# Attention and the first expert layer in one written order, with rope tables built on the chip

## The chip, the cores and the metric

The kernel runs on one core of one Trainium2 chip. The metric is the device time of one execution in microseconds (us). Three runs of the kernel before gave 940.11, 942.00 and 943.37 us; their median is 942.0 us.

A core has five engines that work side by side, each on its own list of instructions in program order: PE multiplies matrices, DVE (VectorE) and ACT (ScalarE) do elementwise work, POOL (GpSimd) does elementwise work more slowly, and SP issues the transfers (DMAs). An instruction that has to wait holds up everything behind it on its engine, and nothing on the others. SBUF is the on-chip memory, PSUM the small memory that PE writes to.

## The reference

Three stages, cut to what is computed:

```
attention, 4 batches x 8 heads, 576 positions, head size 64:
    q, k = rope(q), rope(k)            # x*cos + swapped(x)*(-sin, sin), tables from the position
    attn = softmax(q k^T / 8);  a = attn v
first expert layer: x = a as [2304, 512]
    h = max(x w_in, 0);  x = (h*h) w_out        # w_in [512, 2048], w_out [2048, 512], float64
second expert layer, 8 experts of 512 x 1024 x 512:
    e = argmax(x w_gate + bias[modality]);  gate = its softmax weight
    out[t] = gate[t] * (max(x[t] w1[e], 0) w2[e])
```

## The kernel before, in words

Everything that PE multiplies is split into a high part and a low remainder, so that two or three passes give the precision of float32.

**Attention** (`attention`) works on 16 pairs of heads. For one pair p the steps have short names that the code looks up in the table `fs`:

- `ldq`, `ldk`, `ldv`: loads of q, k, v. q and k come with their halves swapped in a second plane. There is one buffer each for raw q and raw k, so the load of pair p+1 waits until pair p's raw data have been read for the last time.
- `aq`, `bq`, `cq` and `ak`, `bk`, `ck`: rope. Two multiplications with the tables `tab`, each 128x576, and an addition (function `rope`).
- `qh`, `ql`, `kh`, `kl0`, `kl1`: high parts (copies) and low remainders (subtractions). `qd0` to `qd2` and `kd0` to `kd2` move halves between the upper and lower 64 partitions, by a DMA or by a copy on an engine.
- `sc0` to `sc8`: nine tiles of scores on PE, in two PSUM slots. `mx0` to `mx8`: the row maximum of a tile on DVE. `ex0` to `ex8`: exp on ACT, which writes `e` and the row sums. So a score tile waits until the exp of two tiles earlier has left its slot.
- `tr..` and `ev..`: 128x128 transposes of `e` on PE, and the copies that take them out of PSUM. `trrr`, one transpose of the reciprocal row sums, is the only instruction of line 303 and occurs once in a pair. `sa` and `srec` make those reciprocals.
- `pv0`, `pv1`, `u0`, `u1`: attention times v on PE, 20 matmuls each, and the copies of its result; `sev`, `rst`, `rld`, `xn`, `xh`, `xl`, `xr`, `xst` divide by the row sums and store x in DRAM.

**The first expert layer** (`experts`) runs 5 blocks of up to 512 tokens by 16 chunks of 128 hidden columns: `m1` (12 matmuls, `mm1`), `re`, `sq`, `gg`, `gl` (relu, square and remainder on ACT and DVE) and `m2` (12 matmuls, `mm2`). The weights are float64 in DRAM. Each of 32 half chunks i is loaded (`wd`) and turned into two float32 parts by `wx` (ACT, two instructions), `wy` (DVE, two), `wz` (POOL), `wb` (DVE), `wh` (ACT) and `wl` (DVE or POOL). There are four raw buffers and four buffers for the intermediate.

**The order.** Within a pair, tables of due times (`FIRST`, `SECOND`, `THIRD`, `PLAN`, one for pair 0, 1, 2 and 3, and 4 to 15) give each step a time and an engine; a pair's times are shifted by 18 for each pair, and all steps are sorted by time. `TAIL` adds most weight steps of half chunks 0 to 11 and the `m1` of chunks 1, 0 and 2 and the `m2` of chunk 0. From there a loop over units takes over: it emits the `m1` of two chunks ahead, the weight steps of a fixed number per unit (`Weights.slot`) and then the `m2` of its chunk.

At the start the program issues rawk, tabk, rawq and tabq in two halves each, sets whole buffers to zero on POOL (lines 399 to 402), and begins pair 0.

Of the kernel before, what the change touches and what calls it, by code (L numbers as in the profile page):

```python
# [1241 lines left out]
```

## Time and profile before

| | |
|---|---|
| median of three runs | 942.0 us (940.11 to 943.37) |
| the profiled execution's own time | 943.84 us |
| its span, first to last instruction | 942.0 us |
| mean granted TensorE clock | 0.991 of full speed |
| PE busy | 889.0 us, 94% of the span |
| DVE busy | 629.7 us, 67% |
| ACT busy | 471.8 us, 50% |
| POOL busy | 321.3 us, 34% |
| moved by DMA | 122.44 MB |

The busy shares are means over stages with different limits. PE's idle time is 53 us, and the rows below show in which stretches it lies. A profile's times count from the first instruction; what the execution takes beyond its span is 1.84 us.

### The profile page before, as it was taken

The page shows a single profiled execution, that of the slowest core. Times are in us where ns is not written, and L with a number is a line of the kernel's source. Part 1 is how long each engine was busy: PE and PEld are TensorE (multiplying, and loading weights), DVE is VectorE, ACT ScalarE, POOL GpSimd, SP SyncE. Part 2 cuts the span into 40 slices and gives each one's busy share as a digit, 9 for nine tenths or more (in the row PEclk, how much of TensorE's full clock was granted, in tenths as well). Part 3 has the DMA queues.
Part 4 walks back from the last instruction along what each step waited for, and adds up shares of the span by engine and source line. Part 5 has one row for each costly group of instructions (what it writes and reads, how often), then busy time and mean ns, then how long its engine had stood idle before and what let it go on. Part 6 is the DMA issues. An engine that isn't in the chain of part 4 may idle for free. (4 is left out here: it accounts for less than half of the span.)

```text
span 942.0 us, 14580 instructions
## 1 busy us (share of the span) xinstructions
PE 889.0 (94%) x5210; PEld 746.4 (79%) x5210; DVE 629.7 (67%) x1151; ACT 471.8 (50%) x929; POOL 321.3 (34%) x251
## 2 busy tenths in 40 slices
PE   1799999999999999999999999999999999999995
...
GB/s 242 130 158 168 213 176 199 184 201 169 173 104 230 89 183 177 144 102 9 1 79 56 1 1 85 6 1 20 26 202 45 118 230 260 228 224 238 203 92 35
DMA packets 50672, 122.44 MB, mean 130 GB/s; under 512 B 10960, under 2 KB 15072, under 8 KB 50592
## 3 DMA queue, kind: packets, MB, share of 16 engines
...
q8 instruction: 43, 0.70, 0.3%
...
HBM read 93.45 MB, written 15.54 MB: 116 GB/s over the span
## 5 line engine op out<-in xcount | busy, mean ns | idle before, releaser
L665 ACT ACTIVATE r<-h 128x512 f32<-128x512 f32 (+1 forms) x80 | 44.3, 553 | 224.7 <-PE h L659 212.1
L659 PE MATMUL h<-xs,w 128*128 128x512 f32 (+1 forms) x660 | 144.8, 368 | 2.2 <-DVE w L516 2.0
L673 DVE SCALAR_TENSOR_TENSOR h<-h,r 128x512 f32<-128x512 f32 (+1 forms) x80 | 51.6, 644 | 133.3 <-ACT r L665 133.3
L659 PEld LDWEIGHTS h<-xs,w 128*128 128x128 f32 x660 | 115.5, 188 | 25.4 <-DVE w L516 3.7
L270 ACT ACTIVATE e<-sc,nmx 128x576 f32<-128x576 f32 x144 | 106.2, 739 | 54.6 <-DVE nmx L259 53.5
L259 DVE TENSOR_REDUCE nmx<-sc 128x1 f32<-128x576 f32 x144 | 106.7, 753 | 35.6 <-PE sc L254 31.6
L254 PE MATMUL sc<-kh,q 128*128 128x288 f32 (+1 forms) x336 | 98.7, 330 | 33.7 <-ACT q L185 19.2
L693 PE MATMUL y<-w,gh 128*128 128x512 f32 x396 | 122.6, 391 | 0.0
L254 PEld LDWEIGHTS sc<-kh,q 128*128 128x128 f32 x336 | 62.8, 195 | 50.8 <-ACT e L270 24.6
L931 DVE TENSOR_TENSOR w<-eraw,w 128x1024 fp32r<-128x1024 f32 x64 | 78.4, 1225 | 33.8 <-ACT w L930 33.8
L254 PE MATMUL sc<-kl,q 128*128 128x288 f32 (+1 forms) x336 | 90.3, 304 | 0.0
L312 PE MATMUL b<-ident,e 128*128 128x128 f32 x640 | 84.4, 279 | 3.9 <-ACT e L270 3.3
L693 PEld LDWEIGHTS y<-w,gh 128*128 128x128 f32 x396 | 73.3, 188 | 14.4
L580 POOL TENSOR_TENSOR xraw<-xraw,rbs 128x512 f32<-128x512 f32 (+1 forms) x14 | 16.6, 1185 | 196.8 <-DMA rbs<-rD 190.7
L312 PEld LDWEIGHTS b<-ident,e 128*128 128x128 f32 x640 | 75.6, 144 | 4.9 <-ACT e L270 3.7
L693 PE MATMUL y<-w,gl 128*128 128x512 f32 x198 | 77.1, 389 | 0.0
L977 PEld LDWEIGHTS h<-ye,w 128*128 128x128 f32 x576 | 74.0, 189 | 3.7
L977 PE MATMUL h<-ye,w 128*128 128x256 f32 x576 | 74.8, 280 | 0.0
L1000 PE MATMUL y<-w,ge 128*128 128x512 f32 x288 | 74.6, 394 | 0.0
L341 PE MATMUL b<-et,v 128*64 128x288 f32 x512 | 70.0, 412 | 1.0 <-DVE et L187 0.8
...
L930 ACT ACTIVATE w<-eraw 128x1024 fp32r<-128x1024 f32 x64 | 67.3, 1052 | 4.2 <-DMA eraw<-wexp 4.2
(219 smaller groups left out, 1714.4 us busy)
## 6 DMA issues: line engine op xcount, KB each, us to landing
...
```

The lines of the kernel that those rows point to most:

```text
L254: nc.tensor.matmul(out=o[:, x:x + w], lhsT=q[:, hd, q0:q0 + 128], rhs=k[:, hd, y:y + w], start=(n == 0), stop=(n == len(ops) - 1))
L259: nc.vector.tensor_reduce(out=m, in_=sc(p, j)[:, :, 0:HS], axis=AX.XY, op=ALU.max, negate=True)
L270: nc.scalar.activation(out=e(p)[:, o:o + S].rearrange("p (a b) -> p a b", a=2), in_=sc(p, j)[:, :, 0:HS], func=ACTF.Exp, bias=live[p, f"nm ...
L312: nc.tensor.transpose(t[:, i * 128:(i + 1) * 128], x[:, o:o + 128], ident)
L341: nc.tensor.matmul(out=o[64 * hd:64 * hd + 64], lhsT=lhsT, rhs=rhs, start=(c == 0), stop=(c == 4))
L659: nc.tensor.matmul(out=h, lhsT=w[:, a, k * 128:(k + 1) * 128], rhs=xs[b, k][:, c], start=(k == 0 and i == 0), stop=(k == 3 and i == 2))
L673: nc.vector.scalar_tensor_tensor(out=h, in0=h, scalar=W_SC, in1=rs[n], op0=ALU.mult, op1=ALU.mult)
L693: nc.tensor.matmul(out=yp[t], lhsT=g[a][:, t * 128:(t + 1) * 128], rhs=w[:, c, 512:1024], start=(f == 0 and i == 0), stop=(f == NFC - 1 an ...
L930: nc.scalar.activation(out=w[:, 0], in_=r, func=ACTF.Copy)
L931: nc.vector.tensor_tensor(out=w[:, 1], in0=r, in1=f32(w[:, 0]), op=ALU.subtract)
L977: nc.tensor.matmul(out=h, lhsT=w[:, a, k * 128:(k + 1) * 128], rhs=x[:, c], start=(k == 0 and i == 0), stop=(k == 3 and i == 2))
L1000: nc.tensor.matmul(out=yp[s, t], lhsT=g[a][:, t * 128:(t + 1) * 128], rhs=w[:, c, 512:1024], start=(f == 0 and i == 0), stop=(f == EFC - 1 ...
```

## The change

The due-time tables are gone. In their place stands one list, `ORDER`, of 1590 words such as `5.kl0.V`: pair, step and engine, in the order in which they are emitted. Pair 16 stands for the expert layer. The list goes on past attention through all 32 weight half chunks, the `m1` of chunks 0 to 13 and the `m2` of chunks 0 to 11, and the loop over units starts at unit 12 (`HQ`). In the list the `m1` are in the order 4, 1, 0, 2, 3, 5, 7 ahead of the first `m2`, where before three `m1` stood ahead of it.

The rope tables come as one quarter, `tabs`, 64 partitions by 2x576 (288 KB where four transfers of 288 KB were), and the other three quarters are made by four instructions `tab0` to `tab3`, two on DVE and two on ACT. At the start only those parts of the buffers are set to zero that nothing else writes.

The head of the list, and what reads it:

```diff
-        plan = [(t + p * PERIOD, p, name, eng) for p in range(NP)
-                for name, (t, eng) in (FIRST, SECOND, THIRD, THIRD, PLAN)[min(p, 4)].items()
-                if (p or name not in ("ldk", "ldq")) and (p < 4 or name not in BLOCK0)]
-        for t, p, name, eng in sorted(plan, key=lambda z: z[0]):
+ORDER = """
+0.tab2.A 0.tab3.A 0.tab1.V 0.tab0.V 0.ak.V 0.bk.V 0.ck.V 0.aq.V 0.bq.V 0.cq.V 0.kh.A 0.qh.V 0.kd1.A 0.kd0.A 0.ql.V
...
+        for word in ORDER.split():
+            p, name, eng = word.split(".")
+            if int(p) < NP:
+                fs[name](int(p), eng)
+                continue
+            if name in ("open", "bank", "ring"):
+                {"open": early, "bank": banks, "ring": ctx}[name].close()
+            tail(name, eng)
```

```diff
+        def tables(p, eng, n):
+            t = tab["k"][LO]
+            o, i = ((tab["k"][UP, :, 64:S], t[:, :, 0:512]), (tab["k"][UP, :, 0:64], t[:, :, 512:S]),
+                    (tab["q"][LO], t), (tab["q"][UP], t))[n]
...
+        nc.sync.dma_start(out=tab["k"][LO], in_=tabs)
         for x in "kq":
             for c in range(2):
                 nc.sync.dma_start(out=raw(0, x)[:, c], in_=src[x][0, :, c])
-                nc.sync.dma_start(out=tab[x][:, c], in_=table[x][:, c])
-            nc.gpsimd.memset(f32(kl_buf[i]), 0.0)
-            nc.gpsimd.memset(f32(q_buf[i]), 0.0)
+            nc.gpsimd.memset(f32(kl_buf[i][UP, 0]), 0.0)
+            nc.gpsimd.memset(f32(kl_buf[i][LO, 1]), 0.0)
```

Of the buffers, the second `e` moves out of the pool that is closed early, the PSUM of the score tiles is given up at the word `bank`, after the last exp, and the `wb` of odd half chunks writes to SBUF where before, in the loop, it wrote to a PSUM bank.

Three places show what moves. The first is ACT at the start of the program; `tabq<-tabk` builds a table, `wmag<-wraw` and `wraw<-wraw` are weight steps (`wx`), the rest is pair 0. Before:

```order
L483 ACT_TABLE_LOAD
L483 ACTIVATE wmag<-wraw 128x512
L484 ACTIVATE wraw<-wraw 128x512
L185 ACTIVATE kh_85<-rawk 128x576
L185 ACTIVATE kh_85<-kh_85 64x576 x2
L185 ACTIVATE q_83<-rawq 128x576
L185 ACTIVATE q_83<-q_83 64x576
L483 ACTIVATE wmag<-wraw 128x512
L484 ACTIVATE wraw<-wraw 128x512
L185 ACTIVATE kh_85<-kh_85 64x576
L185 ACTIVATE q_83<-ql 64x576
```

Now:

```order
L219 ACT_TABLE_LOAD
L219 ACTIVATE tabq<-tabk 64x1152 x2
L190 ACTIVATE kh_85<-rawk 128x576
L190 ACTIVATE kh_85<-kh_85 64x576 x3
L190 ACTIVATE q_83<-q_83 64x576
L190 ACTIVATE q_83<-ql 64x576
```

No weight step stands ahead of pair 0 any more; two table instructions do.

The second place is POOL in one pair in the middle of attention (`rawq`, `rawk`: rope; `ql`, `kl`: remainders; `e`: `sa`; `wf`: a weight step). Before, one pair takes nine rows:

```order
L201 TENSOR_TENSOR rawq<-rawq,tabq 128x576 x2
L203 TENSOR_TENSOR rawq<-rawq 128x576
L516 TENSOR_TENSOR wf<-wmag,wf 128x512
L190 TENSOR_TENSOR ql<-rawq,q_84 128x576
L201 TENSOR_TENSOR rawk<-rawk,tabk 128x576
L278 TENSOR_SCALAR e_90<-e_90 128x9
L201 TENSOR_TENSOR rawk<-rawk,tabk 128x576
L203 TENSOR_TENSOR rawk<-rawk 128x576
L190 TENSOR_TENSOR kl_88<-rawk,kh_86 64x576
```

Now:

```order
L206 TENSOR_TENSOR rawq<-rawq,tabq 128x576
L206 TENSOR_TENSOR rawq<-rawq 128x576
L486 TENSOR_TENSOR wmag<-wmag,wraw 128x512
L195 TENSOR_TENSOR ql<-rawq,q_84 128x576
L206 TENSOR_TENSOR rawk<-rawk,tabk 128x576 x2
L206 TENSOR_TENSOR rawk<-rawk 128x576
L507 TENSOR_TENSOR wf<-wmag,wf 128x512
```

One rope multiplication of q, the remainder `kl` and `sa` have left POOL.

The third place is DVE at the same point of a pair, between two row maxima (`nmx`) of its scores. Before:

```order
L259 TENSOR_REDUCE nmx<-sc 128x1 x4
L190 TENSOR_TENSOR kl_88<-rawk,kh_86 64x576
L259 TENSOR_REDUCE nmx<-sc 128x1
L187 COPY xo<-b 128x288
L259 TENSOR_REDUCE nmx<-sc 128x1
```

Now:

```order
L271 TENSOR_REDUCE nmx<-sc 128x1 x2
L192 CAST kh_85<-rawk 128x576
L192 COPY rs<-b 9x128
L195 TENSOR_TENSOR kl_87<-rawk,kh_85 64x576
L271 TENSOR_REDUCE nmx<-sc 128x1 x2
L206 TENSOR_TENSOR rawq<-rawq,tabq 128x576
L490 SCALAR_TENSOR_TENSOR wmag<-wraw,wmag 128x512
L195 TENSOR_TENSOR kl_87<-rawk,kh_85 64x576
L490 SCALAR_TENSOR_TENSOR wmag<-wraw,wmag 128x512
L271 TENSOR_REDUCE nmx<-sc 128x1 x2
L192 CAST q_84<-rawq 128x576
```

What left POOL has come to DVE, with the copies `kh` and `qh` from ACT; from DVE to ACT went one copy of 128x288 and some of the transposes' copies.

## Rows read from the trace of the kernel before

**Rows 1.** The page: busy times, and the 40 slices of PE
```profile
PE 889.0 (94%) x5210; PEld 746.4 (79%) x5210; DVE 629.7 (67%) x1151; ACT 471.8 (50%) x929; POOL 321.3 (34%) x251
...
PE   1799999999999999999999999999999999999995
```
**Rows 2.** Busy time by stage: stretch, length, each engine's us and instructions, clock, DMA
```profile
0.00:19.20 19.20, 0.00 (x0) 0.03 (x1) 5.82 (x9) 8.37 (x13) 10.04 (x13) 1.00 0.68 229
19.20:128.30 109.10, 98.18 (x713) 81.13 (x714) 92.61 (x132) 79.77 (x189) 83.44 (x62) 0.97 0.60 173
128.30:293.10 164.80, 157.20 (x1216) 126.80 (x1215) 139.97 (x215) 120.66 (x281) 113.09 (x87) 0.99 0.59 171
293.10:300.10 7.00, 6.01 (x43) 3.04 (x41) 5.50 (x10) 2.29 (x5) 4.14 (x3) 1.00 0.73 226
300.10:420.00 119.90, 115.67 (x501) 93.22 (x501) 91.29 (x154) 67.18 (x117) 52.45 (x37) 1.00 0.48 154
420.00:900.00 480.00, 479.62 (x2585) 413.45 (x2584) 284.61 (x623) 182.91 (x310) 52.30 (x46) 1.00 0.32 101
```
**Rows 3.** Timeline of the start: begin, length, engine, line, idle time before it
```profile
6.21 1.39 POOL L201 TENSOR_TENSOR rawk<-rawk,tabk 128x576 f32<-128x576 f32 x1
6.75 1.47 DVE L201 TENSOR_TENSOR rawk<-rawk,tabk 128x576 f32<-128x576 f32 x1 [5.73 <-DMA tabk<-tabk]
8.32 0.76 DVE L203 TENSOR_TENSOR rawk<-rawk 128x576 f32<-128x576 f32 x1
...
10.16 0.78 DVE L201 TENSOR_TENSOR rawq<-rawq,tabq 128x576 f32<-128x576 f32 x1 [1.09 <-DMA tabq<-tabq]
...
11.94 0.66 ACT L483 ACTIVATE wmag<-wraw 128x512 f32<-128x512 f32 x1 [9.91 <-DMA wraw<-wio]
...
13.05 0.67 ACT L185 ACTIVATE kh<-rawk 128x576 fp32r<-128x576 f32 x1
13.75 1.39 ACT L185 ACTIVATE kh<-kh 64x576 fp32r<-64x576 f32 x2
14.56 1.40 POOL L190 TENSOR_TENSOR kl<-rawk,kh 64x576 fp32r<-64x576 f32 x1 [4.23 <-ACT kh L185]
...
16.55 0.74 DVE L190 TENSOR_TENSOR kl<-rawk,kh 64x576 fp32r<-64x576 f32 x1
...
17.32 0.46 DVE L187 CAST q<-ql 64x576 fp32r<-64x576 f32 x1
...
19.20 0.58 PE L254 MATMUL sc<-kh,q 128*128 128x288 f32 x1 [19.20 <-ACT q L185]
```
**Rows 4.** Timeline of PE: four of the 16 instructions of line 303
```profile
128.33 0.27 PE L303 MATMUL b<-ident,e 128*128 128x128 f32 x1
...
196.65 0.27 PE L303 MATMUL b<-ident,e 128*128 128x128 f32 x1
...
212.19 0.27 PE L303 MATMUL b<-ident,e 128*128 128x128 f32 x1
...
293.14 0.27 PE L303 MATMUL b<-ident,e 128*128 128x128 f32 x1
```
**Rows 5.** Groups of DVE by shape, 100 to 250 us: count, busy us, mean ns, idle before
```profile
L259 DVE TENSOR_REDUCE nmx<-sc 128x1 f32<-128x576 f32 x81 | 60.0, 755 | 13.2 <-PE sc L254 9.8 <-ACT rs L185 1.4
L187 DVE COPY et<-b 128x512 f32<-128x512 f32 x36 | 24.6, 684 | 0.6 <-PE b L312 0.2
L190 DVE TENSOR_TENSOR kl<-rawk,kh 64x576 fp32r<-64x576 f32 x9 | 13.7, 1522 | 0.3
L187 DVE COPY et<-b 128x256 f32<-128x256 f32 x18 | 6.3, 390 | 0.0
L187 DVE COPY xo<-b 128x288 f32<-128x288 f32 x10 | 4.5, 450 | 0.9 <-PE b L341 0.8
```
**Rows 6.** Groups of POOL by shape, 100 to 250 us
```profile
L201 POOL TENSOR_TENSOR rawq<-rawq,tabq 128x576 f32<-128x576 f32 x17 | 24.2, 1443 | 0.0
```
**Rows 7.** Timeline of DVE near the end of attention: one weight step's first instruction
```profile
294.57 0.73 DVE L488 TENSOR_SCALAR wmag<-wmag 128x512 f32<-128x512 f32 x1
```
**Rows 8.** Who waited for whom on PE, 20 to 420 us: total, times, longest
```profile
PE sc L254 <- ACT e L270: 14.2, 14, 2.2
...
PE h L659 <- DVE w L516: 2.0, 4, 0.6
```

More of the change, by code (lines that the diff above doesn't have):

```diff
@@ L36, in f32 @@
     return ap.bitcast(F32)
-PERIOD = 18
-PLAN = {
[20 rows of a table removed]
-}
-FIRST = {
[20 rows of a table removed]
-}
-SECOND = {
[21 rows of a table removed]
-}
-THIRD = {
[21 rows of a table removed]
-}
-TAIL = {
[26 rows of a table removed]
-}
-def attention(tc, qx, kx, v, tabq, tabk, ident, eye, xT, rD, ps, tail=None):
+ORDER = """
+0.tab2.A 0.tab3.A 0.tab1.V 0.tab0.V 0.ak.V 0.bk.V 0.ck.V 0.aq.V 0.bq.V 0.cq.V 0.kh.A 0.qh.V 0.kd1.A 0.kd0.A 0.ql.V
+0.kd2.A 0.qd0.A 0.kl0.V 0.qd1.A 0.sc3.T 0.mx3.V 0.kl1.P 0.sc0.T 0.mx0.V 16.wd0.D 0.ex3.A 1.ldq.D 1.ldk.D 0.ex0.A
+16.wd6.D 16.wd4.D 0.ldv.D 1.ldv.D 16.wd1.D 0.sc2.T 1.bq.P 0.qd2.V 0.sc7.T 0.mx2.V 0.mx7.V 1.aq.V 0.ex2.A 0.ex7.A
@@ new lines @@
+0.sc4.T 1.cq.P 0.sc1.T 0.mx4.V 0.ex4.A 0.mx1.V 0.sc6.T 0.ex1.A 1.qh.A 1.ak.V 1.bk.V 0.mx6.V 1.qd0.A 1.ck.P 0.ex6.A
+0.sc5.T 0.mx5.V 1.ql.V 1.qd1.V 1.kh.A 0.ex5.A 1.kd1.A 0.trm02.T 1.kd0.V 0.trm03.T 0.trm00.T 1.kd2.A 0.sc8.T 0.mx8.V
+1.kl0.P 0.trrk.T 0.ex8.A 0.evrk.V 0.evm02.V 1.kl1.P 1.sc1.T 1.sc3.T 0.evm00.A 0.evm03.A 1.mx1.V 1.ex1.A 1.mx3.V
+0.trm13.T 1.ex3.A 0.sa.P 0.trm12.T 16.wx0.A 1.sc2.T 0.srec.V 0.evm13.V 0.evm12.V 0.trrr.T 0.trm11.T 1.mx2.V 2.ldq.D
+1.ex2.A 1.sc0.T 1.qd2.D 0.trm10.T 1.sc6.T 0.evrr.A 1.mx0.V 2.ldk.D 1.ex0.A 0.evm11.A 1.sc5.T 2.aq.P 2.bq.P 0.trm01.T
@@ new lines @@
+1.trm02.T 2.cq.V 2.ak.V 2.bk.P 1.mx6.V 1.mx5.V 2.qh.A 0.sev.A 2.ck.V 2.ql.V 1.ex6.A 2.qd0.D 3.ldq.D 1.evm02.A
+0.evm01.V 2.kh.A 1.ex5.A 2.kd1.A 1.trm03.T 1.sc8.T 2.kl0.P 1.mx8.V 2.kd0.V 1.ex8.A 2.qd1.D 0.trrq.T 0.evm10.V 0.evrq.A
+2.kl1.P 1.trm00.T 1.sc4.T 1.sc7.T 1.mx7.V 2.kd2.D 0.rst.D 16.wy0.V 3.ldk.D 2.qd2.D 1.ex7.A 0.pv0.T 1.mx4.V 1.ex4.A
+1.evm03.V 2.sc2.T 1.sa.V 2.mx2.V 3.aq.P 3.bq.P 1.srec.V 1.evm00.A 0.u0.A 2.ex2.A 1.trrq.T 2.sc1.T 3.cq.V 3.ak.V 3.bk.P
+1.trm01.T 1.trm12.T 2.sc3.T 0.pv1.T 3.qh.A 1.evm01.A 2.mx1.V 2.mx3.V 3.ck.V 2.ex1.A 3.ql.V 2.ex3.A 0.rld.D 3.qd0.D
@@ new lines @@
+2.sc7.T 1.evrq.V 4.ldq.D 16.wz0.P 2.sc6.T 1.trm10.T 1.evm12.A 3.kh.A 1.trm11.T 3.kd1.A 2.mx7.V 2.mx6.V 3.kl0.P 2.ex7.A
+2.sc4.T 1.trrr.T 2.ex6.A 3.kd0.V 2.sc0.T 3.qd1.D 1.evm11.A 0.u1.A 2.mx4.V 2.ex4.A 1.trm13.T 2.mx0.V 2.ex0.A 1.trrk.T
+3.kl1.P 3.kd2.D 2.sc5.T 4.aq.V 1.evm10.A 2.sc8.T 1.evrr.A 2.mx5.V 0.xr.D 2.trm01.T 1.evm13.V 4.bq.P 2.mx8.V 3.qd2.D
+1.sev.V 4.ldk.D 2.ex5.A 4.cq.P 2.evm01.A 2.ex8.A 3.sc2.T 2.trm13.T 3.mx2.V 4.qh.V 2.trm12.T 2.evm13.V 2.trm02.T
+3.ex2.A 3.sc1.T 1.evrk.A 2.sa.P 2.evm02.A 3.sc3.T 3.mx1.V 4.qd0.D 2.trrq.T 2.trm11.T 3.mx3.V 2.trm00.T 3.ex1.A
@@ new lines @@
+2.evm12.V 2.evm11.V 4.ql.P 2.srec.V 2.ldv.D 4.bk.P 3.ex3.A 3.sc7.T 5.ldq.D 4.ak.P 2.trrk.T 3.sc6.T 2.evrq.A 2.trrr.T
+3.mx7.V 16.wb0.V 4.ck.P 3.mx6.V 2.evrk.A 1.pv1.T 3.ex7.A 16.wx1.A 4.kh.V 2.evrr.V 3.sc4.T 3.ex6.A 1.u1.A 3.sc0.T
+1.pv0.T 4.kd1.D 3.mx4.V 16.wx4.A 4.qd2.D 3.ex4.A 4.kd0.A 3.mx0.V 3.ex0.A 0.xn.P 4.kl0.V 3.sc5.T 5.aq.V 3.sc8.T 0.xh.A
+4.kl1.V 3.mx5.V 1.u0.V 4.kd2.D 3.trm01.T 4.qd1.A 5.bq.P 3.mx8.V 2.trm10.T 5.ldk.D 3.ex5.A 2.sev.A 5.cq.P 2.evm00.V
+3.evm01.A 3.ex8.A 2.evm10.A 4.sc3.T 2.trm03.T 3.trm13.T 5.qh.V 4.mx3.V 4.sc2.T 3.trm12.T 4.ex3.A 3.evm13.V 3.trm02.T
@@ new lines @@
+2.evm03.A 4.sc1.T 3.sa.P 3.evm02.A 1.rst.D 5.qd0.D 3.trrq.T 3.trm11.T 4.mx2.V 3.trm00.T 3.evm12.V 4.mx1.V 3.evm11.V
+5.ql.P 3.srec.V 3.ldv.D 1.rld.D 5.bk.P 4.ex2.A 2.rst.D 6.ldq.D 5.ak.P 4.ex1.A 3.trrk.T 4.sc0.T 3.evrq.A 3.trrr.T
+16.wy4.V 4.sc4.T 2.pv1.T 5.ck.P 4.mx0.V 4.mx4.V 4.ex0.A 3.evrk.A 4.ex4.A 5.kh.V 3.evrr.V 0.xl.V 5.kd1.D 0.xst.D
+5.qd2.D 5.kd0.A 16.wh0.A 4.sc5.T 5.kl0.V 4.sc6.T 4.mx5.V 4.mx6.V 2.pv0.T 4.ex5.A 6.aq.V 5.kl1.V 4.ex6.A 5.kd2.D 2.u0.A
+5.qd1.A 4.sc7.T 6.bq.P 4.ldv.D 3.trm10.T 6.ldk.D 1.xn.V 3.sev.A 6.cq.P 2.rld.D 4.sc8.T 3.evm00.V 4.mx7.V 2.u1.V
@@ new lines @@
+2.xh.A 6.kd1.D 6.qd2.D 2.xl.V 6.kd0.A 5.sc5.T 6.kl0.V 5.sc6.T 5.mx5.V 5.mx6.V 2.xst.D 3.pv0.T 1.xr.D 5.ex5.A 4.pv0.T
+7.aq.V 16.wy2.V 6.kl1.V 5.ex6.A 6.kd2.D 4.u1.A 3.u0.A 6.qd1.A 5.sc7.T 7.bq.P 5.ldv.D 4.rst.D 4.u0.A 7.ldk.D 7.cq.P
+3.rld.D 5.sc8.T 5.mx7.V 3.u1.V 5.trm00.T 4.xr.D 5.trm01.T 5.ex7.A 5.evm00.A 6.sc3.T 5.mx8.V 5.trm13.T 5.trm10.T 7.qh.V
+5.evm01.A 5.trrk.T 6.mx3.V 5.ex8.A 6.sc2.T 5.evm13.V 6.ex3.A 5.trm12.T 5.evrk.A 6.sc1.T 5.trrq.T 5.trm11.T 7.qd0.D
+5.evm10.V 6.mx2.V 5.sa.V 6.mx1.V 5.srec.V 5.trm03.T 7.ql.P 5.evm12.A 7.bk.P 5.trm02.T 6.ex2.A 5.evrq.A 8.ldq.D 7.ak.P
@@ new lines @@
+6.trrq.T 6.trm11.T 8.qd0.D 6.evm10.V 7.mx2.V 6.sa.V 7.mx1.V 6.srec.V 6.trm03.T 8.ql.P 6.evm12.A 8.bk.P 6.trm02.T
+7.ex2.A 6.evrq.A 9.ldq.D 8.ak.P 7.ex1.A 6.evm02.A 6.evm11.V 6.trrr.T 7.sc0.T 6.evm03.V 7.sc4.T 6.evrr.V 8.ck.P 7.mx0.V
+7.mx4.V 7.ex0.A 7.ex4.A 16.wz2.P 8.kh.V 6.sev.V 6.pv1.T 8.kd1.D 16.wb2.V 8.qd2.D 8.kd0.A 7.sc5.T 8.kl0.V 7.sc6.T
+7.mx5.V 7.mx6.V 16.wd5.D 7.ex5.A 6.pv0.T 9.aq.V 16.wx6.A 8.kl1.V 7.ex6.A 8.kd2.D 6.u1.A 8.qd1.A 7.sc7.T 9.bq.P
+16.wy6.V 7.ldv.D 6.rst.D 6.u0.A 9.ldk.D 9.cq.P 7.sc8.T 7.mx7.V 7.trm00.T 6.xr.D 7.trm01.T 7.ex7.A 7.evm00.A 8.sc3.T
@@ new lines @@
+7.mx8.V 7.trm13.T 7.trm10.T 9.qh.V 7.evm01.A 7.trrk.T 8.mx3.V 7.ex8.A 8.sc2.T 7.evm13.V 8.ex3.A 7.trm12.T 7.evrk.A
+8.sc1.T 7.trrq.T 7.trm11.T 9.qd0.D 7.evm10.V 8.mx2.V 7.sa.V 8.mx1.V 7.srec.V 7.trm03.T 9.ql.P 7.evm12.A 9.bk.P
+7.trm02.T 16.wl4.P 8.ex2.A 7.evrq.A 10.ldq.D 9.ak.P 8.ex1.A 7.evm02.A 7.evm11.V 7.trrr.T 8.sc0.T 7.evm03.V 8.sc4.T
+7.evrr.V 9.ck.P 8.mx0.V 8.mx4.V 8.ex0.A 8.ex4.A 9.kh.V 7.sev.V 7.pv1.T 16.wx5.A 9.kd1.D 9.qd2.D 9.kd0.A 16.wh2.A
+8.sc5.T 9.kl0.V 8.sc6.T 8.mx5.V 8.mx6.V 8.ex5.A 7.pv0.T 10.aq.V 9.kl1.V 8.ex6.A 9.kd2.D 16.wy5.V 7.u1.A 9.qd1.A
```

191 lines of the change are left out of this document (123 added, 68 removed), and 108 rows, old and new, of tables (FIRST, PLAN, SECOND, TAIL).

## The prediction

> **What bounds the kernel now.** I read the page first. PE is busy for 889.0 of 942.0 us, and its slices show where it is not: hardly in the first of 40, half in the last, full in between [rows 1]. The last lies behind everything that the change touches. So the change can win only where PE idles ahead of it, and it can lose wherever another engine becomes slower than PE.
>
> Next I cut the span into stages [rows 2]. PE starts at 19.20. From there to the row-sum transpose of the sixth pair (128.33) it idles 109.1 - 98.2 = 10.9 us, over the next ten pairs 164.8 - 157.2 = 7.6 us, and from 300.1 to 420 another 4.2 us. From 420 to 900 it idles 0.4 us of 480, and that stretch keeps its code.
>
> A busy PE can still be slow, so I looked at one instruction that comes once in a pair [rows 4]. From 196.65 to 212.19 a pair took 15.54 us; I use this as PE's floor. The ten pairs up to 293.14 took 164.81 / 10 = 16.48 us each, so 0.94 us of a pair can be won by order. Ten pairs held 1216 matmuls [rows 2], 121.6 each, which makes 15.54 / 121.6 = 0.128 us a matmul. The 713 matmuls of the stretch before would then need 91 us, and took 109.
>
> Who holds PE up is the softmax chain: score tiles waited 14.2 us for the exp that frees their slot, 14 times, up to 2.2 us; exp in turn follows the row maximum on DVE [rows 8, 5]. DVE is busy for 92.6 of 109.1 us and 140.0 of 164.8 us, 85% of both stretches [rows 2]. It is the next bound behind PE, and the question for the new order.
>
> **The start.** Before, three things lie in front of the first score [rows 3]. The rope multiplications wait for the fourth transfer (6.75) and the eighth (10.16). ACT sits idle for 9.91 us in front of a weight step whose data come at 11.94; two such instructions run, and `kh`, whose data were done at 8.32 + 0.76 = 9.1, begins at 13.05. Then high parts, remainders and moves follow each other until 19.20.
>
> Now the loads are five halves of the old size. Four transfers took 10.16 - 6.75 = 3.41 us, 0.85 each, which puts the table at 6.75 - 3 x 0.85 = 4.2 and the last half of q at 7.6. Then on DVE: `tab1` and `tab0`, which no row shows. A one-input instruction over 512 elements took 0.73 [rows 7], and `tab0` has 1024: between 0.73 and 1.46, I take 1.0, and 0.25 for the small `tab1`, so 5.45. Six rope instructions at 0.76 give 10.0, `qh` 0.46 (as the cast of 576 elements at 17.32), `ql` and `kl0` 0.74 each [rows 3]: 11.95. ACT has the two q tables done at 4.2 + 2 x 1.4 = 7.0 (twice the 0.70 of half the 1.39 row), before `aq` needs them at 7.7; then `kh`, three moves, `qd0` and, behind `ql`, `qd1` end at 11.9. On POOL `kl1` runs 1.40 beside the rope work, and a DVE multiplication beside POOL took 1.47 where others took 0.78 [rows 3]: 0.7 more. First score at 12.7, bounds 11.95 and, with all six rope instructions at 1.47, about 17. That is 6.5 us gained; the weight steps that leave come back later on ACT, which is 73% busy there [rows 2]. The smaller zeroing takes POOL off this path altogether. Since `1.ldq` waits for `ql` of pair 0, pair 1 moves forward with it.
>
> **First score to the sixth pair's row-sum transpose.** PE's work ahead of this point is the same but for 4 matmuls. On DVE I counted the words: 27 two-input instructions on SBUF where 14 were, 12 more casts, 5 copies of transposes and one result copy fewer. That is 13 x 0.75 + 12 x 0.46 - 5 x 0.684 - 0.45 = +11.4 us [rows 3, 5], so 104 us of work where 92.6 us were; POOL loses 10 x 1.443 = 14 us [rows 6]. An engine that idled 16.5 us would idle 5. The order can fill PE's holes only as far as DVE lets it; I leave this stretch at 109.1 us, with 97 (PE's 91 and 6 for the first pair, whose tiles can only go at the pace of the exps) and 118 as ends.
>
> **The next ten pairs.** DVE's work is 140.0 / 10 = 14.0 us a pair. It gains `kl0` and `aq` (0.75 each) and `qh` and `kh` (0.46 each), and loses two copies of 0.390 and one of 0.450: +1.2, so 15.2 us, below PE's 15.54. But in this stage `kl1` took 1.522 us [rows 5] and not 0.74. With `kl0` and `aq` at that price it is 16.7 us. POOL, which gives up three of its instructions in a pair, will be in the way less often, so I take the middle, 16.0, and with little idle time left a period of 16.2 us: 10 x (16.48 - 16.2) = 2.8 us gained. Ends: 15.54 and 17.9 (below). ACT rises from 120.7 / 10 = 12.1 us by less than 1.5 and stays hidden.
>
> The row for `kl1` is also where the Trainium skill bears on the case. Its page "SBUF — State Buffer", section "Who interferes with whom", says that a VectorE instruction with two SBUF inputs and a GpSimd instruction that reads SBUF exclude each other: the one that comes second waits for the whole of the first. By that rule `kl0` and `aq` could each wait for a full POOL instruction of 1.443 us, and a pair would come to 15.2 + 2 x 1.44 = 18.1 us, slower than now; at half such a wait it is 16.6. The trace agrees that the two collide (1.522 against 0.74), and its mean extra of 0.78 is near the half.
>
> **The end of attention and the first layer.** I keep the 7.0 us from the last row-sum transpose to the first `m1` [rows 2]. Of the 4.2 us idle up to 420, 2.0 are four waits for weights behind DVE [rows 8]; seven `m1` ahead of the first `m2` give the weight steps some 20 us of cover, so I take 2.0 us off. If DVE had no room here, these waits would come back, 0.6 us each. The remaining weight steps are the same in number.
>
> **Sum.** 12.7 + 109.1 + 162 + 7.0 = 290.8 where 300.1 stood: -9.3, and -2.0 in the first layer: -11.3. The profiled span of 942.0 becomes 930.7; with the 1.84 us outside the span the profiled execution would go from 943.84 to 932.5. The median of the runs equals the span's figure, so I predict 931 us.
>
> **Rivals.**
>
> 1. *PE becomes the only bound.* DVE's collisions go with POOL's load, and the row maxima come when wanted. Then 12.7 + 97 + 155.4 + 7.0 = 272.1, 28 less, and 3 less in the first layer: 911 us. For it: PE did hold 15.54 for single pairs. Against it: DVE would then have to be busy for over 97% of each pair.
>
> 2. *The early start is eaten.* The first pairs are set by DVE, ACT and the arrival of pair 1's data; the new rope work on DVE takes what the start gave, and the stretch grows by the same 6.5 us. Only 2.8 + 2.0 remain: 937 us. For it: the 11.4 us more on DVE just there. Against it: 16.5 us of idle time to put them in.
>
> 3. *DVE becomes the bound (slower).* The place is the middle of attention, behind `kh`, where POOL begins the next pair's rope work while DVE does `kl0`, `aq` and `kl1`. With `kl0` and `aq` at 1.522 and the two casts at twice 0.46 a pair needs 14.0 + 1.2 + 1.54 + 0.92 = 17.7 us, 17.9 with a little idle time; the 13 new instructions of the first stretch at that price make 114 us of work, 118 with idle time. 12.7 + 118 + 179 + 7.0 = 316.7: 16.6 more, 958 us. It decides from a period of 16.48 + 8.5 / 10 = 17.3 us, where start and first layer are paid back. For it: `kl1` in that stage. Against it: POOL has less to do, and its next additions wait for DVE's own results.
>
> **How the numbers follow.** A measurement of this kernel can tell about 0.3% (2.8 us) from no change. My forecast gets 0.40, with a range of its own of 922 to 939; rival 1 gets 0.18, rival 2 0.20, rival 3 0.22. Faster than 939.2: all of rival 1, nearly all of the forecast and two thirds of rival 2, 0.70. Within 0.3%: 0.10. Slower: nearly all of rival 3, 0.20. The range runs from 913 to 950: it leaves out the better half of rival 1 and the worse half of rival 3.
>
> **What would show it.** The first score near 12.7, with no idle time of ACT in front of `kh` but for DVE's rope work. Row-sum transposes 16.2 us apart after the sixth pair; 15.6 would speak for rival 1, over 17.3 for rival 3. DVE's `kl` and `rawq` groups near 1.1 us; at 1.5 rival 3 has its price. DVE busy for over 95% of 109 us in the first stretch. No wait of PE for `w` behind DVE in the first layer. I am wrong altogether if the first score comes after 17, or if another wait (a load held up in SP's queue, a PSUM bank not yet copied out) takes the place of the one on exp; the trace would then show PE idle with that releaser.

## The result: slower, and where

The changed kernel takes 952.54 us (median of 4 runs, 952.28 to 955.74), where the kernel before took 942.68 beside it: ratio 1.011, interval 1.007 to 1.015. I had predicted 931. The profiled span is 950.5 us, 8.5 more than before.

The page of the changed kernel, first the busy times, then PE's 40 slices and its granted clock (to be read beside [rows 1]):

```profile
PE 894.2 (94%) x5210; PEld 749.3 (79%) x5210; DVE 649.4 (68%) x1213; ACT 483.9 (51%) x956; POOL 263.1 (28%) x201
...
PE   3899989898999997799999999999999999999995
...
PEclk9999999999999999799999999999999999999998
```

The first slice is fuller than before, as forecast. But slices 16 and 17 show 7 where [rows 1] have 9, and in the second of them the clock falls to 0.7. Cut into stages (the columns of [rows 2], the first four stages and then the first expert layer in three parts):

```profile
0.00:13.10 13.10, 0.00 (x0) 0.00 (x0) 9.00 (x21) 7.70 (x9) 4.15 (x9) 1.00 0.48 158
13.10:123.60 110.50, 100.72 (x709) 81.42 (x710) 97.80 (x151) 84.04 (x195) 61.93 (x44) 1.00 0.58 173
123.60:293.70 170.10, 159.29 (x1220) 127.75 (x1219) 156.13 (x252) 132.73 (x310) 96.20 (x67) 0.99 0.55 161
293.70:298.90 5.20, 5.20 (x43) 2.83 (x41) 3.47 (x10) 3.19 (x6) 1.05 (x1) 1.00 0.63 233
298.90:374.00 75.10, 74.04 (x326) 60.67 (x324) 53.58 (x83) 45.96 (x82) 30.14 (x23) 1.00 0.40 130
374.00:386.00 12.00, 0.97 (x2) 0.54 (x2) 9.37 (x14) 3.27 (x6) 5.50 (x4) 0.61 0.24 71
386.00:430.00 44.00, 43.37 (x181) 34.83 (x182) 27.92 (x57) 13.38 (x23) 7.02 (x5) 0.95 0.44 136
```

Against [rows 2]: the start is 6.1 us shorter (13.1 for 19.2), the stretch to the sixth pair 1.4 longer (110.5 for 109.1), the next ten pairs 5.3 longer (170.1 for 164.8), the end of attention 1.8 shorter (5.2 for 7.0). So the first `m1` comes only 1.2 us earlier than before, and everything behind it takes 950.5 - 298.9 = 651.6 where it took 942.0 - 300.1 = 641.9: 9.7 us lost, more than the whole difference. In this trace most of it lies in one place: from 374 to 386 PE does 0.97 us of work in 12.

The waits of PE, 10 to 430 us (total, times, longest; [rows 8] before), name it:

```profile
PE sc L266 <- ACT e L282: 18.7, 24, 2.4
...
PE y L685 <- ACT w L504: 11.1, 1, 11.1
PE h L649 <- DVE gl L667: 1.2, 2, 1.0
```

The timeline of the changed kernel around that wait, with rows of ACT, DVE, POOL and PE (begin, length, what ended the idle time before):

```profile
352.31 0.67 ACT L476 ACTIVATE wmag<-wraw 128x512 f32<-128x512 f32 x1
...
360.34 0.60 ACT L655 ACTIVATE r<-h 128x512 f32<-128x512 f32 x1 [6.79 <-PE h L649]
...
368.57 0.66 ACT L476 ACTIVATE wmag<-wraw 128x512 f32<-128x512 f32 x1 [3.31 <-DMA wraw<-wio]
...
373.10 0.43 DVE L481 TENSOR_SCALAR wmag<-wmag 128x512 f32<-128x512 f32 x1 [8.20 <-ACT wmag L476]
...
374.87 4.23 POOL L486 TENSOR_TENSOR wmag<-wmag,wraw 128x512 int32<-128x512 int32 x3 [3.18 <-DVE wmag L482]
...
382.70 1.23 ACT L504 ACTIVATE w<-wmag 128x512 fp32r<-128x512 f32 x2 [9.07 <-DVE wmag L490]
...
385.02 1.52 PE L685 MATMUL y<-w,gh 128*128 128x512 f32 x2 [11.13 <-ACT w L504]
```

Read it from the bottom: an `m2` waits 11.1 us for the high part of a half chunk (25, by the list). That half's batch of four had its first step (`wx`) at 368.57, 16.3 us after the first step of the half before it (352.31). In between ACT idled 6.79 us in front of a `re` that waited for PE's `m1`, and 3.31 us for the load. The list has the loads of this batch among and behind the `wb` of the batch before, three of which ran from 359.51 to 363.10 on DVE: raw buffers are freed and filled a batch at a time. Then the batch goes from engine to engine as a whole: ACT does four `wx`, DVE stands idle 8.2 us and does four `wy`, POOL four `wz`, DVE four `wb`, and ACT idles 9.07 us before `wh`. In the kernel before two halves passed in 6.3 us (first steps at 347.13, 353.42 and 359.70 on its ACT, one half between each two), and its ACT waited less than 1 us for each load. After the wait the first matmuls run slower: two `gh` matmuls take 1.05 us in the timeline up to 390, 0.61 ahead of the wait.

In attention the changed kernel's groups of DVE, 123.6 to 293.7 us, by shape (count, busy us, mean ns, idle before):

```profile
L271 DVE TENSOR_REDUCE nmx<-sc 128x1 f32<-128x576 f32 x87 | 63.5, 752 | 10.4 <-PE sc L266 9.4 <-ACT wraw L477 0.3
...
L195 DVE TENSOR_TENSOR kl<-rawk,kh 64x576 fp32r<-64x576 f32 x18 | 18.8, 1043 | 0.3
...
L192 DVE CAST kh<-rawk 128x576 fp32r<-128x576 f32 x9 | 6.4, 711 | 0.3 <-POOL rawk L206 0.3
L206 DVE TENSOR_TENSOR rawq<-rawq,tabq 128x576 f32<-128x576 f32 x8 | 6.0, 750 | 0.0
L290 DVE TENSOR_SCALAR e<-e 128x9 f32<-128x9 f32 x10 | 5.7, 574 | 0.0
```

`kl` costs 1.04 us, near the 1.1 that I had expected; the cast costs 0.71 and not 0.46, and `sa`, an addition over nine elements, 0.57. The rope multiplication `aq` (`rawq`) costs 0.75, and not the 1.1 that I had expected for it too. DVE idles 10.4 us in front of row maxima, nearly all of it for score tiles, and PE in this stretch waits 10.2 us, nine times, for the exp behind a row maximum (6.7 us, six times, before). Two rows of PE's timeline (line 315, the row-sum transpose of the sixth and of the last pair, as in [rows 4]) give the ten periods, 170.1 / 10 = 17.0 us. Single periods are far from alike: 14.9 to 20.1 us here, the longest right behind the sixth pair, and 14.2 to 19.5 before.

```profile
123.61 0.27 PE L315 MATMUL b<-ident,e 128*128 128x128 f32 x1
...
293.71 0.27 PE L315 MATMUL b<-ident,e 128*128 128x128 f32 x1
```

### The profile page after: what moved, and what is told of

Same layout as the page of the kernel before. It is cut to its first block, busy times and chain, and to the rows that moved or that the text cites. A ratio compares the mean times of both kernels' runs of the same rounds, so it can differ in the third digit from the quotient of the medians.

```text
span 950.5 us, 14463 instructions
## 1 busy us (share of the span) xinstructions
PE 894.2 (94%) x5210; PEld 749.3 (79%) x5210; DVE 649.4 (68%) x1213; ACT 483.9 (51%) x956; POOL 263.1 (28%) x201
## 5 line engine op out<-in xcount | busy, mean ns | idle before, releaser
L685 PE MATMUL y<-w,gh 128*128 128x512 f32 x396 | 124.6, 396 | 11.1 <-ACT w L504 11.1
L266 PE MATMUL sc<-kh,q 128*128 128x288 f32 (+1 forms) x336 | 100.0, 335 | 32.1 <-ACT e L282 18.7
L271 DVE TENSOR_REDUCE nmx<-sc 128x1 f32<-128x576 f32 x144 | 105.6, 752 | 17.8 <-PE sc L266 15.6
L266 PE MATMUL sc<-kl,q 128*128 128x288 f32 (+2 forms) x336 | 91.5, 308 | 0.0
L697 DVE SCALAR_TENSOR_TENSOR junk<-ysb,wgb 128x512 f32<-128x512 f32 x96 | 64.3, 725 | 0.0
```

The source lines that it names most:

```text
L266: nc.tensor.matmul(out=o[:, x:x + w], lhsT=q[:, hd, q0:q0 + 128], rhs=k[:, hd, y:y + w], start=(n == 0), stop=(n == len(ops) - 1))
L271: nc.vector.tensor_reduce(out=m, in_=sc(p, j)[:, :, 0:HS], axis=AX.XY, op=ALU.max, negate=True)
L685: nc.tensor.matmul(out=yp[t], lhsT=g[a][:, t * 128:(t + 1) * 128], rhs=w[:, c, 512:1024], start=(begin and i == 0), stop=(f == NFC - 1 and ...
L697: nc.vector.scalar_tensor_tensor(out=junk, in0=ysb[j], scalar=1.0, in1=wgb[e], op0=ALU.mult, op1=ALU.mult, accum_out=lg[:, j, e:e + 1])
```

## The experiments

Two questions: what made the first layer late (its list, in batches, or the price of its steps), and where the 6 us of the start went (price or order of DVE's work in attention). All times are medians, with the ratio to runs of the kernel before on the same chip; what is said of stages comes from one profiled execution of each kernel.

**e1_batch25: half chunk 25 ahead of its batch.** The end of the list:

```diff
-16.wx31.A 16.wh29.A 16.wx30.A 16.wl29.P 16.wx25.A 16.wx27.A 16.gg13.V 16.wy27.V 16.wy31.V ...
+16.wx25.A 16.wh29.A 16.wy25.V 16.gg13.V 16.gg12.V 16.wz25.P 16.sq12.A 16.wb25.V 16.gl13.V 16.wh25.A ...
```

> The changed kernel with only the end of its list rewritten: of the last four half chunks of weights, number 25 is prepared first on every engine, and not behind 31, 30 and 27. Theory A (PE's 11.1 us wait at 374 us is for half chunk 25, whose data lay ready while ACT worked through 31 and 30): the wait goes or falls below 2 us, with it the slow clock behind it, 13 to 14 us in all: 937 to 941 us. Rival (the weight chain as a whole is late, limited by four raw buffers and the loads): the wait moves to the next chunk, at least 7 us of it stay, 947 to 953 us.

Measured: 949.69 us, ratio 1.0084 (1.0055 to 1.0112), span 947.6. The wait of 11.1 us is gone; PE now waits at several later places, of which these are three rows:

```profile
PE h L649 <- DVE xs L578: 2.4, 1, 2.4
PE h L649 <- ACT xs L577: 1.5, 1, 1.5
PE h L649 <- ACT w L504: 1.4, 1, 1.4
```

First `m1` to the end is 947.6 - 299.16 = 648.4, 3.2 less than 651.6 and still 6.5 over the kernel before. One half's place in the list was not the cause of the whole loss; that the halves as a whole come late is the reading that is left, and e5 tests it.

**e2_pool and e3_act: half of the moved work off DVE.** In pairs 4 to 15 e2 gives `kl0`, `aq` and `sa` back to POOL, e3 gives `kh` and `qh` back to ACT, at the same places of the list:

```diff
-12.kl0.V ... 13.aq.V ... 11.sa.V
+12.kl0.P ... 13.aq.P ... 11.sa.P
```

```diff
-12.kh.V ... 13.qh.V
+12.kh.A ... 13.qh.A
```

> The changed kernel with kl0, aq and sa of pairs 4 to 15 back on POOL, nothing else. Theory A (DVE's added work sets the period of 17.0 us in the middle of attention): DVE falls from 92% to about 85% busy there, the ten periods shorten from 170.1 us to 165 or less, 5 us or more off the time. Rival (the words' order sets it, where weight steps stand ahead of row maxima): the ten periods stay within 2 us of 170, and the time within 3 us of the changed kernel's.

> The changed kernel with the copies kh and qh of pairs 4 to 15 back on ACT, nothing else. Theory A (DVE's work sets the period): DVE loses about 1.3 us a pair, ACT gains 1.35 us on 13.3; the ten periods shorten by 4 to 8 us. Rival (order): within 2 us of 170. Second rival (ACT is then the bound, its exps come late): the ten periods grow.

Measured: 958.52 us (ratio 1.0178, 1.0141 to 1.0216) and 957.11 us (1.0156, 1.0129 to 1.0184). The ten periods stay at 17.1 us in both. The stage of the ten pairs (columns as above), e2 first:

```profile
127.00:298.00 171.00, 159.47 (x1220) 127.91 (x1219) 149.78 (x225) 132.62 (x310) 127.22 (x94) 0.99 0.54 162
```

```profile
124.80:295.90 171.10, 160.41 (x1220) 126.40 (x1219) 144.50 (x235) 141.77 (x327) 96.23 (x66) 1.00 0.53 159
```

DVE is down to 149.8 and 144.5 us, and no period is won. In e2 the price of what stays rises: `kl` costs 1.64 us beside the busier POOL. So DVE's busy time by itself does not set the period, as the rival on order had it. The times are 6.0 and 4.6 us over the changed kernel's, more than the 3 that this rival allowed for e2; the sixth pair already ends 3.4 and 1.2 us later than there (126.99 and 124.80).

**e4_start: the kernel before, its three early weight steps later.**

```diff
-"wx2": (-674.0967, "A"), "wx0": (-619.2397, "A"), "wx1": (-607.7358, "A")
+"wx2": (-528.0967, "A"), "wx0": (-504.2397, "A"), "wx1": (-475.7358, "A")
```

> The kernel before with only three ACT weight steps (wx of half chunks 2, 0, 1) moved from in front of pair 0's copies to behind its first exps. The first score should move from 19.2 to about 15, since ACT no longer waits for the weights' data. If an early start passes through to the end, 938 to 939 us; if the first pairs' own work on DVE and ACT eats it (rival 2 of the prediction), within 2 us of 942, with the sixth pair's row-sum transpose still near 128.

Measured: 940.35 us, ratio 0.9985 (0.996 to 1.001). The first score comes at 15.75 (3.45 earlier than before), the first `m1` at 296.68 (3.4 earlier). The median lies within the second forecast and can't tell this from no change, but the trace is that of the first: the sixth pair is at 126.09, and in the old order the early start reaches the end of attention whole.

**e5_rolling: the first layer's words in a rolling order.** The list is kept up to the last pair; behind it the steps of each half follow the one before it:

```diff
+16.wx22.A 16.wy22.V 16.wz22.P 16.wb21.V 16.wd25.D 16.wh20.A 16.wl20.P 16.m17.T 16.re7.A 16.sq7.A 16.gg7.V 16.gl7.V
+16.wx23.A 16.wy23.V 16.wz23.P 16.wb22.V 16.wd26.D 16.wh21.A 16.wl21.V 16.m25.T ...
```

> The changed kernel with its list kept up to the last pair; the words behind it, the first layer's, are written in a rolling order: two half chunks a chunk of PE's work, each half's steps one half behind the other (first step of half i, sign of i-1, load of i+3, high and low part of i-2), where the list starts the steps in batches of four halves. Half chunks 14, 15, 12 and 18, which the list began early, become 11, 12, 13 and 14. Instructions are the same in number. Theory A, the batches: four raw buffers are filled, worked on and freed together, so that the first steps of a batch start 15 to 20 us after those of the one before, 4 us a half where the kernel before took 3.1; in the rolling order no wait of PE for weights over 1 us is left, first m1 to the end falls from 651.6 to 643 or 644, and the time from 952.5 to 944 or 945. Rival B, the price: the weight steps on DVE cost 1.03 (low part) and 0.83 us (sign) beside POOL, whatever their order, because the sign of odd halves no longer goes to a PSUM bank; then the halves still come too late, first m1 to the end stays at 648 or more, and the time at 949 or more.

Measured: 941.36 us, ratio 0.9986 (0.9971 to 1.0002): 11 us less than the changed kernel with as many words in the list. Besides the order, eight of the low parts (`wl`) go from DVE to POOL in it and four from POOL to DVE, and `m1` and `m2` are mixed in another order. First `m1` to the end is 939.2 - 299.84 = 639.4, below the 641.9 of the kernel before. First steps of halves on ACT in its timeline now come every 3.1 or 3.8 us:

```profile
357.38 0.69 ACT L475 ACTIVATE wmag<-wraw 128x512 f32<-128x512 f32 x1 [1.79 <-POOL w L506]
360.45 0.68 ACT L475 ACTIVATE wmag<-wraw 128x512 f32<-128x512 f32 x1
364.25 0.67 ACT L475 ACTIVATE wmag<-wraw 128x512 f32<-128x512 f32 x1 [1.77 <-POOL w L506]
```

and PE waits for no weight; the largest wait left behind the first `m1` is this row:

```profile
PE y L684 <- DVE gl L666: 2.7, 3, 1.4
```

The prices did not fall, as a group of DVE from 300 to 385 us shows (1.03 us in the changed kernel's):

```profile
L506 DVE TENSOR_TENSOR w<-wmag,w 128x512 fp32r<-128x512 f32 x11 | 18.5, 1678 | 0.0
```

So the order behind the last pair cost the first layer its time, and rival B falls. That it was the batches in that order is what the waits of ACT and DVE above say; no run changes the batches alone.

**e6_nobank: the kernel before without the PSUM bank of odd halves.**

```diff
-        wts.bank = bank
```

> The kernel before with one line less: the sign step of odd half chunks writes back to SBUF, as in the changed kernel, and not to a PSUM bank. Theory A (the batches alone cost the first layer its time): within 2 us of the kernel before, 941 to 945, although DVE's low parts rise from 0.68 to about 1.0 us. Rival B (the price of DVE's weight steps beside POOL): 11 low parts at 1.035 in place of 0.684 are 3.9 us on the engine that PE waits for, and their lateness is added up; 946 to 950.

Measured: 946.53 us, ratio 1.0035 (1.0017 to 1.0053), some 3.3 us slower: rival B, at the lower end of what it expected. In the trace first `m1` to the end takes 948.0 - 301.62 = 646.4, 4.5 more than before, and PE's waits for `w` in it are 5.4 us, put down to POOL's low parts, where they were 2.0, put down to DVE's. Rival B expected them behind DVE; that DVE's slower steps make POOL's late is likely and not shown. (Its start, which the edit does not touch, is 0.6 us later than before: so far do single executions differ.) The low part on DVE, 300 to 385 us, in the kernel before and then in e6:

```profile
L516 DVE TENSOR_TENSOR w<-wbank,w 128x512 fp32r<-128x512 f32 x11 | 7.5, 684 | 0.0
```

```profile
L516 DVE TENSOR_TENSOR w<-wmag,w 128x512 fp32r<-128x512 f32 x10 | 18.0, 1803 | 0.0
```

With one input in PSUM it takes 0.68 us, with both in SBUF 1.80 in this order (1.03 in the changed kernel's). I had described this line of the change and put no price on it.

**e9_rollbank: e5 with the bank again.**

```diff
+        if self.ring and i % 2:
+            self.mag[i] = self.bank([128, 512], "wbank").bitcast(I32)
```

> As e5_rolling (941.4), and behind the word ring the sign step of odd half chunks writes to a PSUM bank, as in the kernel before. Theory A, the two costs add up: e6_nobank lost 3.5 us by giving the bank up, so the bank gives some 3 us here too: 938 to 939. Rival B, one cost covers the other: e5_rolling begins the first layer with two half chunks more than the kernel before, its PE waits for no weights over 1 us, and the dearer steps on DVE hide in that lead; 941 to 942.

Measured: 939.53 us, ratio 0.9966 (0.995 to 0.9982). That is 1.8 us under e5 by the medians, between the two theories, and too little to tell them apart: first `m1` to the end is 937.6 - 298.75 = 638.9, 0.5 less than in e5. This version is faster than both kernels, by some 3 us than the one before.

**e7_dveorder: the row maxima ahead.** On top of e1, pairs 4 to 15, words of DVE:

```diff
-16.wb6 11.mx0 11.mx4 12.kh 10.sev 12.kl0 11.mx5 11.mx6 13.aq 16.wb3 12.kl1 11.mx7 11.mx8 13.qh
+11.mx0 11.mx4 12.kh 10.sev 11.mx5 11.mx6 12.kl0 13.aq 12.kl1 16.wb6 11.mx7 11.mx8 13.qh 16.wb3
```

> As e1_batch25 (949.7), and in pairs 4 to 15 DVE's words are put in another order: the row maxima 5 and 6 stand ahead of kl0, where kl0 and weight words stood ahead of them, and the weight words stand behind qh or kl1, where they stood ahead of maxima 0 and 4 or 5 and 6. Nothing changes its engine. Theory A, the order: PE waits for an exp whose row maximum stands behind such a word on DVE, so the ten periods after the sixth pair fall from 17.0 to 16.5 or less, and the time by 5 us or more, to 944 or 945. Rival B, the load: DVE is busy for 92% and late on average, so what is moved from ahead of two maxima is late in front of two others; the ten periods stay at 16.9 to 17.1, the time within 2 us of 949.7.

Measured: 950.82 us, ratio 1.0078 (1.0062 to 1.0093). The ten periods take 168.2 us, 2 less than in e1, but the sixth pair ends 3 us later (126.63). The time is rival B's, and the period of 16.8 lies between the two theories: what is moved away from one maximum is late elsewhere.

**e8_start: the changed start in the old order.** The kernel before with the quarter table, the small zeroing and pair 0's steps as the changed kernel has them:

```diff
+    "tab2": (-700.0, "A"), "tab3": (-699.0, "A"), "tab1": (-698.0, "V"), "tab0": (-697.0, "V"), "ak": (-696.0, "V"), ...
```

> The kernel before with the start of the changed one: the quarter table and its copies on chip, the small zeroing, pair 0's rope work and high parts as the changed kernel has them, and the three weight steps later as in e4_start. Everything from pair 1 on stands in the order of the kernel before. Theory A, an early start passes through in that order: e4_start scored at 15.75 and its first m1 came 3.4 us earlier than before, as much as its score; here the first score comes at about 13.1, 6 us earlier than before, the first m1 at 294 to 295, and the time is 937 to 938. Rival B, the start is eaten whatever the order, since pair 1 waits for its own loads and rope work: first m1 at 296 to 297 as in e4_start, 940.

Measured: 938.91 us, ratio 0.996 (0.9939 to 0.9981). First score at 13.03, sixth pair at 123.09, last at 287.76, first `m1` at 294.72, 5.4 us earlier than before. Theory A: of the 6.2 us of the start 5.4 arrive at the first `m1` in the trace, and the medians differ by 3.6. So the stretch to the sixth pair takes 110 us in either order, and it is the ten pairs that differ, 164.7 here and 170.1 in the changed list.

**e10_map: the old engines in the new list.** On e5, pairs 4 to 15:

```diff
-kl0.V aq.V sa.V kh.V qh.V kd0.A qd1.A u1.A
+kl0.P aq.P sa.P kh.A qh.A kd0.D qd1.D u1.V
```

> As e5_rolling (941.4), and in pairs 4 to 15 the words that the change gave to other engines go back to the engines of the kernel before, at the places that the list has for them: kl0, aq and sa to POOL, kh and qh to ACT, kd0 and qd1 to DMAs, u1 to DVE. Theory A, the load as a whole: e2_pool and e3_act took one half of it off DVE each, and gave POOL or ACT more; together with the moves taken off ACT the period falls from 17.1 to 16.6 or less, and the time by 4 us or more, to 937. Rival B, the order: the list was made for other durations, and a word that is late holds up what stands behind it whatever its engine, the kernel before differs in the order in which scores, transposes and exps follow each other on PE and ACT; the period stays at 16.9 or above, the time at 940 or more.

Measured: 966.42 us, ratio 1.027 (1.0247 to 1.0294); the ten periods are 18.7 us. Theory A falls. The result is on rival B's side of its bounds, but 25 us over e5 is more than it said: this list, written for one set of engines, does not serve the other.

**e11_nopool: POOL's rope work left out in pairs 4 to 15.** On e9:

```diff
-14.bq.P ... 14.cq.P ... 14.bk.P ... 14.ak.P ... 14.ck.P
```

> As e9_rollbank (939.5; ten periods after the sixth pair 17.0 us), and in pairs 4 to 15 POOL's five rope instructions (ak, bk, ck, bq, cq) are left out, so that q and k of these pairs are not rotated as the reference has them; the order of all that stays is the same. Theory A, collisions: DVE's instructions stretch beside POOL's (kl 1.04 us on average where it took 0.74 alone); without them kl takes 0.75, a weight word on DVE never over 1 us, DVE is busy for under 86% of the ten periods, and a period takes 16.2 us or less: 8 us or more gained, 931 or less. Rival B, the list: the order of scores, maxima and exps alone holds the period; it stays at 16.8 or more and the time at 937 or more.

Measured: 922.06 us, ratio 0.9776 (0.9749 to 0.9804), 17.5 us less than e9. The ten pairs, e9 first, then e11:

```profile
123.30:293.60 170.30, 159.45 (x1221) 127.72 (x1218) 156.30 (x252) 132.89 (x310) 95.63 (x67) 0.99 0.55 161
```

```profile
119.30:276.20 156.90, 156.16 (x1221) 126.08 (x1219) 139.25 (x251) 132.10 (x310) 31.33 (x23) 1.00 0.59 175
```

DVE does as many instructions (251 for 252) in 17 us less, and the period falls to 15.7 us, where PE is busy 99.5% of the time. Four groups of DVE in e11, 123.3 to 293 us, show where DVE's time went:

```profile
L266 DVE TENSOR_REDUCE nmx<-sc 128x1 f32<-128x576 f32 x85 | 62.6, 754 | 14.0 <-PE sc L261 11.7 <-ACT et L185 0.7 <-ACT kh L185 0.4
...
L190 DVE TENSOR_TENSOR kl<-rawk,kh 64x576 fp32r<-64x576 f32 x18 | 13.4, 747 | 0.3
...
L187 DVE CAST kh<-rawk 128x576 fp32r<-128x576 f32 x8 | 3.6, 450 | 0.0
L285 DVE TENSOR_SCALAR e<-e 128x9 f32<-128x9 f32 x10 | 2.5, 246 | 0.0
```

What PE waited for in the ten pairs, e9 (123.3 to 293.6 us) and then e11 (119.3 to 276.2):

```profile
PE sc L265 <- ACT e L281: 9.8, 9, 2.2
```

```profile
PE sc L261 <- ACT e L277: 0.2, 1, 0.2
```

`kl` falls to 0.75 and the cast to 0.45, near the 0.74 and 0.46 of [rows 3], and the short addition to 0.25; the row maximum stays. The periods now lie between 15.0 and 16.1 us. Theory A: without POOL's work the list holds PE's floor. One thing is mixed in: without the additions `ck` and `cq` the high parts do not wait for POOL either, and the raw buffers may come free earlier. In the changed kernel the wait of `kh` for POOL is 0.3 us in its group above and PE waits there for exps alone, so I put the gain down to the collisions; no run parts the two.

**e12_spread: weight words in POOL's pause.** On e8, three of the words that move:

```diff
-"wy6": (-160.1285, "V"), "wb6": (-144.7472, "V"), "wy7": (-127.5613, "V")
+"wy6": (-157.4, "V"), "wb6": (-139.4, "V"), "wy7": (-121.4, "V")
```

> As e8_start (938.9), and the weight words of DVE between the fourth and the last pair (wy, wb and one wl) are due in the pause that POOL makes ahead of ql, behind row maximum 8, where most were due among POOL's rope instructions; the POOL and ACT words that follow them move with them. Theory A, collisions: in e8_start one such word took 4.33 us and another 3.12 beside two POOL instructions in a row, and pairs with a weight word there took 17.6 to 19.6 us where the others took 15.5; in the pause they cost 0.43 to 0.7, and the time falls by 3 us or more, to 935 or 936. Rival B: in the pause they hold up copies of transposes and row maximum 3, and PE waits there instead: within 2 us of 938.9.

Measured: 944.69 us, ratio 1.0025 (1.0008 to 1.0041), slower than e8. The price did fall: the integer shift of `wy`, 120 to 300 us, in e8 and then in e12:

```profile
L505 DVE TENSOR_SCALAR wmag<-wmag 128x512 int32<-128x512 int32 x8 | 8.4, 1050 | 0.3
```

```profile
L505 DVE TENSOR_SCALAR wmag<-wmag 128x512 int32<-128x512 int32 x7 | 5.1, 724 | 0.2
```

and still the ten pairs take 166.0 us for 164.7, and the sixth pair comes 2.4 us later (125.50). In the ten pairs PE now waits 1.9 us, four times, for copies of transposes, a wait that e8 does not have there. Rival B named this place; it expected less loss, and what holds up the pairs ahead is not shown.

## Why the prediction was wrong, step by step

- **The start** (12.7): 13.13. Right, in part by luck: the table was down at 4.71 and not at 4.2, and `tab1` and `tab0` together took 0.82 us and not 1.25. The 0.4 us more are `ql`, which took 1.84 us beside POOL's `kl1`, as these rows of the changed kernel's timeline show; I had put 0.7 us of collision on the rope work, it was 1.1 on `ql`.

```profile
10.00 1.68 POOL L195 TENSOR_TENSOR kl<-rawk,kh 64x576 fp32r<-64x576 f32 x1 [6.85 <-DVE rawq L206]
10.45 1.84 DVE L195 TENSOR_TENSOR ql<-rawq,q 128x576 fp32r<-128x576 f32 x1
```

- **First score to the sixth pair** (109.1 kept): 110.5, and 110.0 in e8's other order. Right. Rival 2, the early start eaten here, did not happen. The count of DVE's new instructions was right (151 for 132), their price was not: DVE was busy for 97.8 us and not 104, 89% and not over 95%.
- **The ten pairs** (period 16.2): 17.0, 8.1 us too little in the sum. The busy time of DVE that I forecast, 16.0 us a pair, was near the 15.6 measured, but by luck: `sa`, 0.57 us a pair, and eleven more weight instructions in these ten pairs (28 for 17) were not in my sum, while `kl` fell from 1.52 to 1.04 and `aq` cost 0.75. The step that failed is "with little idle time left": PE at 94% and DVE at 92% wait for each other's results (row maxima for score tiles, score tiles for exps), and DVE kept 1.4 us a pair of idle time where I had given it 0.2. Rival 3 had the mechanism in part (e11; `kl` and the casts pay, `aq` does not), but its period was 17.9; the 17.3 from which it decides was not reached, so it alone did not make the kernel slower.
- **The rule on the shared port.** I weighed it for instructions with two SBUF inputs alone. By the rows of the changed kernel and of e11 casts and one-input instructions pay too (0.71 for 0.45, 0.57 for 0.25), while the row maximum does not (0.752 us beside POOL, 0.754 without its rope work). `aq`, with two SBUF inputs, costs 0.75 in both, since POOL stands idle beside it: eight of POOL's rope instructions wait 29.6 us in all for `aq` in the changed kernel's ten pairs. The Trainium skill says just this in "SBUF — State Buffer", section "Who interferes with whom": copies, casts and `tensor_scalar` can enter modes that take the shared pair, `tensor_reduce` on trn2 never does. The rows of the cast, the short addition and the row maximum agree. The same section of the Trainium skill has an instruction with at most one SBUF input, outside those modes, free of GpSimd; e6's 0.68 against 1.80 us agrees.
- **End of attention** (7.0 kept): 5.2, 1.8 better.
- **The first layer** (-2.0): +9.7. This is the step that made the sign wrong. I asked only whether DVE had room, priced its failure at 0.6 us a wait, and wrote that the remaining weight steps were the same in number. They were, but not in order and not in price: e5's order, with 12 of the low parts on other engines, gives back 12.2 us, and e6 shows 3.3 us for the bank in the old order. There was no wait for `w` behind DVE, as I had said; one wait of 11.1 us for `w` behind ACT took its place, which no rival named. My sign of being wrong altogether speaks of another wait in place of the one on exp; the waits on exp stayed (18.7 us for 14.2), and this one came on top.
- **Sum.** Span forecast 930.7, measured 950.5: 8.1 from the ten pairs and 11.7 from the first layer are the 19.8; the other steps cancel (0.4 + 1.4 - 1.8).

What stays open is why a period of the old order needs less with dearer single instructions (`kl` 1.52 us in [rows 5]). It has less work on DVE (140.0 us for 156.1), but e3, with 144.5, stays at 17.1; e7 and e10 show that neither the words around the maxima nor the engines alone explain it.
